# Two loads moved behind a DMA turning, the last remainder tile moved behind a visit's groups, and output banks dealt by element, in a fused attention and two-layer kernel on one Trainium2 core

## The chip, the cores and the metric

The kernel runs on one core of one Trainium2 chip. The metric is the device time of one execution in microseconds (us). The core has a matrix engine, TensorE (PE in the profile, its weight loads PEld), and three more that compute: VectorE (DVE), ScalarE (ACT) and GpSimd (POOL). SyncE (SP) only issues DMAs. POOL issues DMAs too. Each engine works through its own list of instructions in order and waits on semaphores for the others. PE writes its results to PSUM, which has eight banks; DVE and ACT read them there.

## The reference

The kernel computes an attention with normalised queries and keys and passes the result through two matrix products with a leaky ReLU between them.

```python
# batch 8, heads 12, sequence 448, head size 64; d_model 768, d_ff 2048
q_n = q / (np.linalg.norm(q, axis=-1, keepdims=True) + 1e-06)
k_n = k / (np.linalg.norm(k, axis=-1, keepdims=True) + 1e-06)
scores = np.matmul(q_n, k_n.transpose(0, 1, 3, 2)) / tau          # tau = 0.1
scores = scores - np.max(scores, axis=-1, keepdims=True)
attn = np.exp(scores)
attn = attn / (np.sum(attn, axis=-1, keepdims=True) + 1e-09)
attn_out = np.matmul(attn, v)
x = attn_out.transpose(0, 2, 1, 3).reshape(3584, 768)
h = x @ w_in                                                       # 768 x 2048
out = np.maximum(0.01 * h, h) @ w_out                              # 2048 x 768
```

## The kernel before

**Units of work.** The 12 heads of a batch entry are taken two at a time: a pair s, six to a batch entry, 48 in all. A pair's 448 positions are three full tiles of 128 and a remainder of 64. The remainders of two neighbouring pairs share one tile. Two pairs make an element j, three elements to a batch entry. The two matrix products go over chunks of tokens: two batch entries are 896 columns, cut into a chunk of 384 (three tiles of 128, the even chunks) and one of 512 (four tiles, the odd chunks). There are eight chunks.

**A pair's way.** `load_qk(s)` issues four DMAs from SyncE (two of 192 KB, two of 32 KB) into one of four buffers. `squares(s)` squares them on GpSimd, behind `hold`, a one-element copy that makes GpSimd wait until a given pair has been normalised. `sums(s)` reduces the squares on VectorE, `roots(s)` takes the root on ScalarE, `normalise(s)` multiplies on VectorE. `transposes(s)` turns the pair: by PE for s below 10, and from s = 10 on (`DMA_FROM`) with one transposing DMA from SyncE, L259, into one of five buffers `qkT`. `norm(s)` is roots, normalise and transposes, and then the loads of a later pair, the hold, and the squares of pair s + 2.

**A chunk's way.** `firsts(b)` multiplies chunk b by `w_in` (L388) and ScalarE applies the leaky ReLU (L395), giving `hT`. Then `visit(b)` multiplies `hT` by `w_out` (L460) in `two_groups`: two output groups at once, in the two row halves of the PE array, 2 x 16 steps `n` of one pair of matmuls, into the two banks of a bank pair; VectorE then copies both banks out (L470), and SyncE stores the tile when both of its halves are there. Between these steps `visit` places the score tiles of batch entry b + 1 (`key_tiles`, L284, each into a bank pair, exponential on ScalarE, L296): the schedules `three` and `four` say after which step of a group a tile comes. A remainder tile (`ki == 3`) is made of four matmuls in 64 x 64 parts of the array. Two of the three remainder tiles of a batch entry stand ahead of the groups, the last one right after the last full tile, inside the last `two_groups`. After the visit, `attend_batch(b + 1)` computes the attention: `attend_two` for two elements together (remainder parts first, L311, in 64 x 32 parts of the array; then totals and products, L324, 128 x 32), `attend` for the third. `reciprocals` (L343, L344) are on ScalarE, `scale` (L365) on VectorE; its output xT is what the next `firsts` multiplies.

**What sets the order.** The order is written out by hand (`manual_schedule`): every engine gets its instructions in the order of the calls. Semaphores are put in by the framework. SyncE's DMAs take eight completion counters in turn, so each DMA also waits until the one eight before it has landed. Banks are dealt by `banks`: of the pairs that are not kept, the one whose last deal or return is the oldest. In `two_groups` the pair is kept until its copies are issued.

In the visit of chunk 0, the attention's batch entry 1 is being prepared, and the pairs of batch entry 2 begin to be loaded: `norm(10)` comes at the end of `firsts(0)` and `norm(11)` after step 26 of the first `two_groups`.

Of the kernel before, what the change touches and what calls it, by code (L numbers as in the profile page):

```python
# [16 lines left out]
def kernel(  # L17
# [10 lines left out]
    nc = tc.nc  # L28
# [10 lines left out]
    NQ = NPAIR // 2  # L39
    KT = D_model // 128  # L40
    MT = D_ff // 128
    HALF = D_model // 2
# [33 lines left out]
    def banks(count, keep=None, which=None):  # L76
        lo, hi = (0, 8) if not deals["apart"] else (0, 4) if count == 2 else (4, 8)
        x = which if which is not None else min(
            (i for i in range(lo, hi, count) if not set(range(i, i + count)) & set(sum(kept.values(), []))),
            key=lambda i: max(age[i : i + count]),  # L80
        )
        deals["n"] += 1
        age[x : x + count] = [deals["n"]] * count
        if keep:
            kept[keep] = list(range(x, x + count))
        return ps[:, x] if count == 1 else ps[:, x : x + count]
# [31 lines left out]
    def main(x, b, h0, nh):  # L118
        return x[b, h0 : h0 + nh, 0:MAIN].rearrange("h (p t) d -> p h t d", t=3)
# [19 lines left out]
    def load_qk(s):  # L139
        if s >= NSLOT:  # L140
            return
        b, h0 = s // NPAIR, 2 * (s % NPAIR)
        both = ldp.tile([128, 2, 7, D], F32, name="qk")
        nc.sync.dma_start(out=both[:, :, 0:3], in_=main(q, b, h0, 2))
        nc.sync.dma_start(out=both[:, :, 4:7], in_=main(k, b, h0, 2))
        for i, x in enumerate((q, k)):
            nc.sync.dma_start(
                out=both[64 * i : 64 * i + 64, :, 3],
                in_=x[b, h0 : h0 + 2, MAIN:S].rearrange("h p d -> p h d"),
            )  # L150
        raw[s] = (both[:, :, 0:4], both[:, :, 4:7])
# [23 lines left out]
    def squares(s, engs=(gp, gp)):  # L175
        if s >= NSLOT:
            return
        tiles = []
        for x, eng, name in zip(raw[s], engs, ("sq0", "sq1")):
            sq = sqp.tile(list(x.shape), F32, name=name)  # L180
            if eng is nc.scalar:
                nc.scalar.activation(sq, x, func=AF.Square)
            else:
                eng.tensor_tensor(sq, x, x, op=ALU.mult)  # L184
            tiles.append(sq)
        sqs[s] = tiles
# [22 lines left out]
    def behind(eng, ins, why):  # L209

        tc.add_manual_dep(
            eng.nop().ins, ins.ins.name,
            mybir.DependencyInfo(mybir.DependencyClass.Sync, mybir.DependencyReason.DATA),
            reason=why,
        )
# [56 lines left out]
    def key_tiles(which):  # L272

        tiles = []
        for s, ki in which:
            sc = banks(2)
            tiles.append(sc)
            for i in range(2 if ki == 3 else 1):
                x = qkT[s - 1 + (i ^ s // 2 % NQ % 2)] if ki == 3 else qkT[s]
                for a in range(2):  # L280
                    rows = slice(64 * a, 64 * a + 64)
                    out = sc[64 * i : 64 * i + 64] if ki == 3 else sc
                    c0, c1 = (448, 512) if ki == 3 else (512 + 128 * ki, 640 + 128 * ki)
                    nc.tensor.matmul(  # L284
                        out=out[:, a, :S], lhsT=x[rows, c0:c1], rhs=x[rows, 0:S],
                        start=True, stop=True,
                    )
        for (s, ki), sc in zip(which, tiles):
            if ki == 3:
                pr[s // 2] = prp.tile([128, 2, S], BF16, name="pr")  # L290
                dst = pr[s // 2]
            else:
                if s not in pe:
                    pe[s] = pep.tile([128, 3, 2, S], BF16, name="pe")
                dst = pe[s][:, ki]
            nc.scalar.activation(out=dst, in_=sc[:, :, :S], func=AF.Exp, scale=inv_tau)  # L296
# [52 lines left out]
    def products(j, e, po=None, begun=False):  # L349
        b, jj = divmod(j, NQ)  # L350
        if po is None:
            po = banks(1, (j, e))
        pos[j, e] = po
        vm = vb[j].rearrange("p h t (d e) -> p h t e d", e=2)
        vr = vrb[b % 2].rearrange("p j g (d e) -> p j g e d", e=2)
        strip_products(
            j, po, lambda g, ki: vm[:, g, ki, e], None if begun else lambda g: vr[:, jj, g, e]
        )
# [15 lines left out]
    def chunk_cols(c):  # L374
        return (0, MAIN) if c % 2 == 0 else (MAIN, 512)
# [25 lines left out]
    osb = {}  # L401
# [41 lines left out]

    halves_done = {}

    def two_groups(c, two):

        po2 = banks(2, ("rows", c, two))  # L450
        last = {}
        for n in range(2):
            before, last = last, {}
            for m in range(MT):
                for h in range(2):
                    rows, i = slice(64 * h, 64 * h + 64), h ^ n
                    ts, half = two[i]
                    if n == 1 and m == 0:
                        behind(nc.tensor, before[i], "the other rows' products in this bank")
                    last[i] = nc.tensor.matmul(  # L460
                        out=po2[:, i, :HALF],
                        lhsT=hT[c][rows, m, ts * 128 : (ts + 1) * 128],
                        rhs=w_out_sb[rows, m, half * HALF : (half + 1) * HALF],
                        start=(n == 0 and m == 0), stop=(n == 1 and m == MT - 1),
                    )
                yield
        for i, (ts, half) in enumerate(two):
            if (c, ts) not in osb:
                osb[c, ts] = osp.tile([128, D_model], F32, name="osb")
            nc.vector.tensor_copy(  # L470
                out=osb[c, ts][:, half * HALF : (half + 1) * HALF], in_=po2[:, i, :HALF]
            )
            halves_done[c, ts] = halves_done.get((c, ts), 0) + 1
            if halves_done[c, ts] == 2:
                store(osb[c, ts], c, chunk_cols(c)[0] + ts * 128, 0, D_model)
        given_back(("rows", c, two))
# [38 lines left out]
    def hold(x):  # L515
        seen = smp.tile([128, 1], F32, name="seen")
        gp.tensor_copy(out=seen, in_=x)  # L517
# [154 lines left out]
    def attend_two(j):  # L672
        two = (j, j + 1)
        sm = banks(2)
        po = [banks(2) for _ in two]
        vr = vrb[j // NQ % 2].rearrange("p j g (d e) -> p j g e d", e=2)
        rem_products(two, [sm[:, i] for i in range(2)], lambda j, g, rows: ones[rows])
        for e in range(2):
            rem_products(
                two, [x[:, e] for x in po], lambda j, g, rows, e=e: vr[rows, j % NQ, g, e]  # L680
            )
        for i, j in enumerate(two):
            totals(j, sm[:, i])
        for j, x in zip(two, po):
            for e in range(2):
                products(j, e, x[:, e], True)
            for e in range(2):
                scale(j, e)

# [11 lines left out]
    def norm(s, transposed=True):  # L701
        if s >= NSLOT:
            return
        roots(s)
        normalise(s)
        if transposed:
            transposes(s)
        if 9 <= s < 12:
            load_qk(s + 2)
        elif s not in (7, 8):  # L710
            load_qk(s + 4)
        hold(qn[s][:, 6, 0, 0:1])
        squares(s + 2)

    def firsts(b, begun, between):
# [9 lines left out]
    def visit(b, order, norms, between):  # L725


        s0 = (b + 1) * NPAIR
        tiles = [(s0 + p, ki) for p in range(NPAIR) for ki in range(3)]
        key_tiles([(s0 + 1, 3), (s0 + 3, 3)])  # L730
        for i, two in enumerate(order):
            after = between[i == len(order) - 1]
            for n, _ in enumerate(two_groups(b, two), 1):
                for _ in range(after.get(n, 0)):
                    key_tiles([tiles.pop(0)])
                if not tiles and s0 + 5 not in ended:
                    ended.add(s0 + 5)
                    key_tiles([(s0 + 5, 3)])
                for fn in norms.get((i, n), ()):
                    fn()  # L740
        assert not tiles

    ended = set()
    three = ({5: 1, 11: 1, 16: 2, 21: 1, 27: 1}, {3: 1, 7: 1, 11: 1, 16: 2, 20: 1})
    four = ({5: 1, 11: 1, 16: 2, 24: 1}, {6: 1, 16: 2})

# [17 lines left out]
    for b in range(B):  # L764
# [6 lines left out]
        order = [((ts, 0), (ts, 1)) for ts in range(tokens)]  # L771
        if b == 0:
            order = [((0, 0), (1, 0)), ((2, 0), (0, 1)), ((1, 1), (2, 1))]
# [12 lines left out]
        s = ready  # L786
# [57 lines left out]
```

## Time and profile before

| what | value |
| --- | --- |
| median of 3 runs | 411.54 us (411.3 to 411.54) |
| the profiled execution | 411.49 us, of it 409.7 us from first to last instruction |
| PE busy | 400.1 us, 98% of the span |
| ACT, DVE, POOL busy | 259.0, 193.4 and 140.7 us |
| L388, products with w_in | 148.1 us in 768 matmuls |
| L460, products with w_out in `two_groups` | 143.3 us in 1536 matmuls of half the rows |
| L284, scores | 54.8 us in 384 matmuls |
| L470, copies of `two_groups` on VectorE | 48, 552 ns each |
| DMA turnings, L259 | 38, median 3.0 us from issue to landing |

A busy time of PE is not PE at its peak: records of matmuls overlap, and matmuls in different parts of the array run together. The columns of the order of time, shown below, are: start in us from the span's start, duration, engine, line, operation, what it writes and reads, sizes, how many; in brackets how long the engine was idle before it, and what ended that.

### The profile page before, as it was taken

How to read it: one execution, taken by the hardware profiler on the slowest of the kernel's cores; microseconds unless marked ns; L12 is line 12 of the kernel's file. 1: busy time of each engine (PE TensorE's matmuls, PEld its weight loads, DVE VectorE, ACT ScalarE, POOL GpSimd, SP SyncE). 2: the span in 40 equal slices, each digit the busy share in tenths (PEclk: the TensorE clock that was granted, in tenths of full speed). 3: DMA queues.
4: the chain of work that ended last, by engine and by line, in shares of the span. 5: the costliest groups of instructions: out<-in, count | busy, mean ns of one | idle time of the engine just before them, and what ended most of it. 6: DMA issues, size and time to landing. Idle time of an engine off the chain costs nothing.

```text
span 409.7 us, 10108 instructions
## 1 busy us (share of the span) xinstructions
PE 400.1 (98%) x4096; PEld 213.8 (52%) x4096; DVE 193.4 (47%) x412; ACT 259.0 (63%) x448; POOL 140.7 (34%) x216
## 2 busy tenths in 40 slices
PE   7899998999999999999999999999999999999996
PEld 3335655544555655544555555544555555554564
DVE  5987850762644734365453625257261645130021
ACT  4996597546865579745875569745775559844300
POOL 4995461282323423254140624055231530000000
PEclk9999999999999999999999999999999999999999
DMA  7999999596495839277485868587385833210023
GB/s 170 263 214 217 221 178 205 169 179 160 109 202 94 152 77 195 84 114 156 107 186 122 120 139 141 132 113 136 92 194 126 119 82 63 62 41 2 0 77 78
DMA packets 104175, 54.21 MB, mean 132 GB/s; under 512 B 70016, under 2 KB 99072, under 8 KB 104128
## 3 DMA queue, kind: packets, MB, share of 16 engines
q1 hardware_dynamic: 78064, 41.04, 44.1%
q0 software_dynamic: 25216, 12.00, 22.8%
q8 instruction: 32, 0.52, 0.6%
q10 hardware_dynamic: 848, 0.52, 0.4%
q14 instruction: 15, 0.12, 0.1%
HBM read 45.61 MB, written 11.01 MB: 138 GB/s over the span
## 4 chain that ended last, share of the span: by engine, by line
PE 82%; DMA 11%; POOL 3%; DVE 1%; issue 1%; ACT 0%; POOLq 0%
PE ps L388 32%; PE ps L460 28%; PE ps L324 10%; DMA w_out_sb<-in_moe_w_out_dram 7%; PE ps L284 6%; PE ps L425 5%; DMA raw<-in_k_dram 2%; DMA qkT<-qn 2%; POOL sq L184 2%; PE ps L311 1%; DVE qn L227 1%; POOL w_out_sb L113 1%; DVE r L223 0%; POOL seen L517 0%; POOL w_in_sb L106 0%
## 5 line engine op out<-in xcount | busy, mean ns | idle before, releaser
L388 PE MATMUL ps<-xT,w_in_sb 128*128 128x384 bf16 (+1 forms) x768 | 148.1, 353 | 0.0
L460 PE MATMUL ps<-w_out_sb,hT 64*128 64x384 bf16 x1536 | 143.3, 323 | 0.3 <-DMA w_out_sb<-in_moe_w_out_dram 0.3
L296 ACT ACTIVATE pe<-ps 128x896 bf16<-128x896 f32 x144 | 123.3, 919 | 21.7 <-PE ps L284 20.0
L388 PEld LDWEIGHTS <-w_in_sb 128*128 128x128 bf16 x768 | 74.1, 98 | 71.8 <-issue 4.0
L395 ACT ACTIVATE hT<-ps 128x384 bf16<-128x384 f32 (+1 forms) x128 | 67.3, 543 | 69.6 <-PE ps L388 69.2
L460 PEld LDWEIGHTS <-hT 64*128 64x128 bf16 x1536 | 74.7, 94 | 54.8 <-issue 4.0
L184 POOL TENSOR_TENSOR sq<-qk 128x512 f32<-128x512 f32 x84 | 77.1, 939 | 18.0 <-DMA qk<-in_k_dram 17.0
L470 DVE COPY osb<-ps 128x384 f32<-128x384 f32 x48 | 24.5, 552 | 78.4 <-PE ps L460 45.2
L284 PE MATMUL ps<-qkT 64*128 64x448 bf16 (+1 forms) x384 | 54.8, 354 | 3.2 <-DMA qkT<-qn 1.6
L195 DVE TENSOR_REDUCE ss<-sq 128x6 f32<-128x384 f32 (+1 forms) x95 | 54.5, 610 | 3.0 <-POOL sq L184 2.9
L517 POOL CAST seen<-qn 128x1 f32<-128x1 bf16 x48 | 9.0, 188 | 130.0 <-DVE qn L227 125.3
L227 DVE TENSOR_TENSOR qn<-qk,r 128x512 bf16<-128x512 f32 x84 | 50.5, 642 | 2.0 <-DVE r L223 0.6
L222 DVE TENSOR_SCALAR ss<-ss 128x14 f32<-128x14 f32 x46 | 10.5, 227 | 66.9 <-ACT ss L203 66.8
L365 DVE TENSOR_TENSOR xT<-ps,rb 128x448 bf16<-128x448 f32 x48 | 27.7, 619 | 20.5 <-ACT rb L344 20.3
L162 POOL DMA_DIRECT2D v_b<-in_v_dram x24 | 18.7, 784 | 54.2 <-PE ps L324 54.2
L324 PE MATMUL ps<-pe,v_b 128*32 128x448 bf16 x576 | 32.0, 353 | 0.0
L284 PEld LDWEIGHTS <-qkT 64*128 64x128 bf16 (+1 forms) x384 | 17.0, 96 | 22.8 <-issue 8.8
L343 ACT ACTIVATE rb<-ps 128x448 f32<-128x448 f32 x24 | 12.9, 537 | 22.2 <-PE ps L324 21.2
L431 DVE COPY osb<-ps 128x384 f32<-128x384 f32 (+1 forms) x9 | 4.6, 512 | 36.6 <-issue 22.6
L296 ACT ACTIVATE pr<-ps 128x896 bf16<-128x896 f32 x24 | 21.3, 922 | 0.2 <-PE ps L284 0.2
L324 PEld LDWEIGHTS <-v_b 128*32 128x32 bf16 x576 | 15.2, 97 | 11.8 <-issue 0.6
L425 PE MATMUL ps<-w_out_sb,hT 128*128 128x384 bf16 (+1 forms) x144 | 21.0, 308 | 0.0
(51 smaller groups left out, 196.2 us busy)
## 6 DMA issues: line engine op xcount, KB each, us to landing
qk<-in_q_dram SPq DMA_DIRECT2D x42, 192.0 KB, 3.4
qk<-in_k_dram SPq DMA_DIRECT2D x42, 192.0 KB, 3.4
out_dram<-osb SPq DMA_DIRECT2D x30, 192.0 KB, 3.0
v_b<-in_v_dram POOLq DMA_DIRECT2D x24, 192.0 KB, 4.9
out_dram<-osb SPq DMA_DIRECT2D x12, 384.0 KB, 2.7
w_in_sb<-in_moe_w_in_dram POOLq DMA_DIRECT2D x4, 768.0 KB, 11.8
w_out_sb<-in_moe_w_out_dram POOLq DMA_DIRECT2D x2, 768.0 KB, 21.8
w_out_sb<-in_moe_w_out_dram POOLq DMA_DIRECT2D x4, 384.0 KB, 25.2
```

Source lines behind the costliest of these rows:

```text
L184: eng.tensor_tensor(sq, x, x, op=ALU.mult)
L195: nc.vector.tensor_reduce(o.rearrange("p (h t) -> p h t", h=2), sqs[s][i], axis=AX.X, op=ALU.add)
L227: scalings[s] = nc.vector.tensor_tensor(qn[s][:, lo:hi], x.rearrange("p h t d -> p t h d"), r[:, r0 : r0 + 2 * nt].rearrange("p (h t) -> p ...
L284: nc.tensor.matmul(out=out[:, a, :S], lhsT=x[rows, c0:c1], rhs=x[rows, 0:S], start=True, stop=True,)
L296: nc.scalar.activation(out=dst, in_=sc[:, :, :S], func=AF.Exp, scale=inv_tau)
L324: nc.tensor.matmul(out=x[32 * g : 32 * g + 32, :S], lhsT=weights(g, ki) if ki < 3 else rem(g), rhs=pe[s][:, ki, a, :] if ki < 3 else pr[j] ...
L365: nc.vector.tensor_tensor(xT[m][:, 2 * jj + e, half * S : (half + 1) * S], pos.pop((j, e))[:, :S], rbs[j], op=ALU.mult,)
L388: nc.tensor.matmul(out=pm[:, :n], lhsT=w_in_sb[:, kt, m * 128 : (m + 1) * 128], rhs=xT[c // 2][:, kt, c0 : c0 + n], start=(kt == 0), stop= ...
L395: nc.scalar.activation(out=hT[c][:, m, :n], in_=pms.pop((c, m))[:, :n], func=AF.Prelu, alpha=0.01)
L425: nc.tensor.matmul(out=po2[:, :n], lhsT=hT[c][:, m, ts * 128 : (ts + 1) * 128], rhs=w_out_sb[:, m, lo : lo + n], start=(m == 0), stop=(m = ...
L460: last[i] = nc.tensor.matmul(out=po2[:, i, :HALF], lhsT=hT[c][rows, m, ts * 128 : (ts + 1) * 128], rhs=w_out_sb[rows, m, half * HALF : (ha ...
L470: nc.vector.tensor_copy(out=osb[c, ts][:, half * HALF : (half + 1) * HALF], in_=po2[:, i, :HALF])
```

## The change

**Loads.** `norm(10)` ends after the turning of pair 10: its loads of pair 12, its hold and its squares of pair 12 are left out there. `norm(11)` then loads pairs 12 and 13 one after the other, behind the turning of pair 11, and squares pair 12 ahead of pair 13. One hold is left out for good.

**Remainder tile.** The last remainder tile of a visit, which stood inside the last `two_groups`, comes behind all groups of the visit, after the last copies have been issued and the bank pair is back in the deal. It holds for the seven visits.

**Copies.** In the last `two_groups` of a visit, the first of the two copies is made by ScalarE and the second by VectorE; before, VectorE made both.

**Banks in `attend_two`.** Of the two bank pairs for products, one held both halves e of the first element and the other those of the second. Now one holds half e = 0 of both elements and the other half e = 1 of both.

```diff
-    def two_groups(c, two):
+    def two_groups(c, two, last):
...
-            nc.vector.tensor_copy(
-                out=osb[c, ts][:, half * HALF : (half + 1) * HALF], in_=po2[:, i, :HALF]
-            )
+            copy = nc.scalar.copy if last and i == 0 else nc.vector.tensor_copy
+            copy(out=osb[c, ts][:, half * HALF : (half + 1) * HALF], in_=po2[:, i, :HALF])
...
-        po = [banks(2) for _ in two]
+        po = [banks(2) for e in range(2)]
...
             rem_products(
-                two, [x[:, e] for x in po], lambda j, g, rows, e=e: vr[rows, j % NQ, g, e]
+                two, [po[e][:, i] for i in range(2)], lambda j, g, rows, e=e: vr[rows, j % NQ, g, e]
             )
...
-        for j, x in zip(two, po):
+        for i, j in enumerate(two):
             for e in range(2):
-                products(j, e, x[:, e], True)
+                products(j, e, po[e][:, i], True)
...
-        if 9 <= s < 12:
-            load_qk(s + 2)
+        if s == 10:
+            return
+        if s == 11:
+            load_qk(12)
+            load_qk(13)
         elif s not in (7, 8):
-            load_qk(s + 4)
+            load_qk(s + (2 if s == 9 else 4))
         hold(qn[s][:, 6, 0, 0:1])
+        if s == 11:
+            squares(12)
         squares(s + 2)
...
-            for n, _ in enumerate(two_groups(b, two), 1):
+            for n, _ in enumerate(two_groups(b, two, i == len(order) - 1), 1):
                 for _ in range(after.get(n, 0)):
                     key_tiles([tiles.pop(0)])
-                if not tiles and s0 + 5 not in ended:
-                    ended.add(s0 + 5)
-                    key_tiles([(s0 + 5, 3)])
                 for fn in norms.get((i, n), ()):
                     fn()
         assert not tiles
+        key_tiles([(s0 + 5, 3)])
```

More of the change, by code (lines that the diff above doesn't have):

```diff
@@ L444 @@
     halves_done = {}
-    def two_groups(c, two):
+    def two_groups(c, two, last):
         po2 = banks(2, ("rows", c, two))
-        last = {}
+        done = {}
         for n in range(2):
-            before, last = last, {}
+            before, done = done, {}
             for m in range(MT):
@@ L459, in two_groups @@
                         behind(nc.tensor, before[i], "the other rows' products in this bank")
-                    last[i] = nc.tensor.matmul(
+                    done[i] = nc.tensor.matmul(
                         out=po2[:, i, :HALF],
@@ L741, in visit @@
         assert not tiles
-    ended = set()
+        key_tiles([(s0 + 5, 3)])
     three = ({5: 1, 11: 1, 16: 2, 21: 1, 27: 1}, {3: 1, 7: 1, 11: 1, 16: 2, 20: 1})
```

## The prediction, made before the changed kernel was run

> **What bounds the kernel now.** I read the page's first two parts, then the waits, then the order of time around the one long wait, then the order of time at the end of an ordinary visit. By the page, TensorE (PE) works 400.1 of 409.7 us at the full granted clock; the other engines are far from full, and DMA is full only in the first 70 us.
>
> ```profile
> span 409.7 us, 10108 instructions
> PE 400.1 (98%) x4096; PEld 213.8 (52%) x4096; DVE 193.4 (47%) x412; ACT 259.0 (63%) x448; POOL 140.7 (34%) x216
> PE   7899998999999999999999999999999999999996
> PEclk9999999999999999999999999999999999999999
> DMA  7999999596495839277485868587385833210023
> ```
>
> So only what leaves PE idle can be won. Of the waits that end a PE idle time, the longest is a single one, for a DMA turning (the transpose of L259):
>
> ```profile
> PE ps L284 <- DMA qkT<-qn: 1.6, 1, 1.6
> PE ps L508 <- DVE warm L491: 1.5, 1, 1.5
> ```
>
> The second is the start-up, which the change leaves alone. The first stands in the visit of chunk 0. I call pair s's four loads "loads s" and its turning "turning s" (s counts from 0: the 12th pair is s = 11). SPq is SyncE's queue:
>
> ```profile
> 53.19 1.35 SPq L259 DMA_TRANSPOSE qkT<-qn  x1
> 54.65 0.51 SPq L144 DMA_DIRECT2D qk<-in_q_dram  x1
> ...
> 56.49 0.70 SPq L147 DMA_DIRECT2D qk<-in_k_dram  x1
> ...
> 59.57 2.64 SPq L259 DMA_TRANSPOSE qkT<-qn  x1
> ...
> 66.31 1.82 POOL L184 TENSOR_TENSOR sq<-qk 128x512 f32<-128x512 f32 x2 [6.35 <-DMA qk<-in_k_dram]
> 66.89 1.11 PE L460 MATMUL ps<-w_out_sb,hT 64*128 64x384 bf16 x10
> 69.62 0.55 PE L284 MATMUL ps<-qkT 64*128 64x448 bf16 x4 [1.61 <-DMA qkT<-qn]
> 71.68 1.82 POOL L184 TENSOR_TENSOR sq<-qk 128x512 f32<-128x512 f32 x2 [3.43 <-DMA qk<-in_k_dram]
> ```
>
> Turning 10 goes out at 53.19, loads 12 behind it, turning 11 at 59.57. By the tile's view both turnings land 9.9 to 10.0 us after their issue: 63.1 and 69.6. The squares of s = 12 start at 66.31, when loads 12 have landed. PE needs turning 11 when its last pair ends: the record of a matmul is about 0.16 us longer than the pace at which the next one follows, so PE could have gone on at 68.00 - 0.16 = 67.85 and loses 69.62 - 67.85 = 1.77 us.
>
> The end of an ordinary visit (chunk 1):
>
> ```profile
> 122.41 0.85 PE L284 MATMUL ps<-qkT 64*128 64x448 bf16 x8
> 122.88 0.11 PEld L284 LDWEIGHTS <-qkT 64*64 64x64 bf16 x4 [0.37 <-issue]
> 123.20 2.77 PE L460 MATMUL ps<-w_out_sb,hT 64*128 64x384 bf16 x32
> 125.91 0.38 PE L311 MATMUL ps<-pr,ones 64*32 64x448 bf16 x8
> 126.07 1.02 DVE L470 COPY osb<-ps 128x384 f32<-128x384 f32 x2 [5.22 <-ACT pr L296]
> 126.11 0.56 PE L311 MATMUL ps<-pr,v_rem 64*32 64x448 bf16 x16
> 126.60 1.32 PE L324 MATMUL ps<-pe,ones 128*32 128x448 bf16 x24
> ```
>
> Tiles that lie beside each other in the array run together as a set. A set of 448 columns takes 0.19 us (an L284 pair at 120.60, L460 at 120.79, both in 64*128), a pair of 384 columns 0.163. What is more than that is lost where the array's tile shape changes: two L284 pairs (0.38) begin at 122.41, the remainder tile (64*64) at 122.88: 0.09 lost. From there to L460 it is 0.32, 0.13 lost. Sixteen L460 pairs take 2.60 and end at 125.80, L311 begins at 125.91: 0.10 lost.
>
> **The change part by part.**
>
> *Loads behind the turning.* In the built program SyncE's order is turning 10, turning 11, loads 12, loads 13, the first store. Turning 11 still waits for its normalised rows (SyncE's wait ended at 59.5 on DVE), so it goes out at 59.57. What changes is what lies ahead of it in the queue: turning 10 (landed 63.1) in place of loads 12 (landed 66.2). It landed 69.6 - 66.2 = 3.4 us after the work ahead; behind turning 10 that gives 63.1 + 3.4 = 66.5, which is 1.35 us before PE wants it. Bounds: 3.0 us after issue (the page's median of 38 turnings), and 9.9 us, turning 10's own time, though loads 11, ahead of it, had landed by 53.2. I take 66.5, whose row is the same turning in the same traffic: the wait goes, -1.77 us. [...]
>
> What moves: four DMAs of loads 12 (2.5 us of issue) and four of loads 13, from 54.65 and 62.31 to 62.3 and 64.8 or so, and the first store (65.93) behind them, to about 67.3 or when loads 12 have landed, whose completion counter it reuses. The output tile that this store empties is wanted again at 107.5. Loads 12 then land where they stood behind turning 10 before, 3.1 us after the turning: 69.6, loads 13 at 71.5 as now, since the queue holds the same work. POOL loses one 0.26 us cast (the hold of s = 10) and squares s = 12 at 69.7 to 71.5. VectorE sums them after its last copy, at about 71.9 in the new time (74.5 now), and its next work, the first scaling (76.06 now, about 74.2 then), waits for ScalarE anyway. So loads 12 may land at 71.7 with no effect, and PE is reached 1.5 us beyond that (the four scalings end at 78.35, L388 starts at 79.85). If this cover went, each us would cost one. The remainder rows of v, third of four transfers, landed at 70.5; attention will want them at 73.56 - 1.77 - 0.12 = 71.7: cover 1.2 us, same price.
>
> *Remainder tile behind the groups*, seven visits. Three changes of shape (0.09 + 0.13 + 0.10 = 0.32) become two: into 64*64 (0.09 to 0.10) and from 64*64 to 64*32, which this trace does not have. Its nearest rows are the changes beside it, 0.09 to 0.13; zero is the lower end. I take 0.10: 0.20 in all, -0.12 a visit, -0.84 us. [...] ScalarE's exponential of this tile moves behind the groups too (0.92 us); it is wanted by the totals of the third element, some 4.6 us later, and the logarithm of the first totals comes 2.1 us after the last pair has begun, when that exponential has ended (0.37 + 0.49 + 0.93 = 1.8). Cover 0.3 us; beyond it ScalarE would delay the scalings, which have 1.5 us of their own.
>
> *Banks dealt by element, one copy on ScalarE.* The oldest banks now go to the remainder tile, so the third set of L311 (element half e = 1) falls on the banks that the last group has just filled: a new wait of PE, for a copy on ScalarE and one on VectorE. Count from the start of the last L460 pair, 125.65: PE comes to that set after 0.163 + 0.10 (into 64*64) + 0.19 + 0.10 (into 64*32) + 0.20 + 0.19 = 0.94. VectorE's copy starts at 126.07 (0.42) and takes 0.55 (552 ns is the mean of L470); PE follows DVE after 0.06 (a DVE copy ended 24.88, PE started 24.94): 1.03. ScalarE's copy is not in the trace; the nearest row, L395 of the same 128x384, has 490 ns, and ScalarE starts 0.05 after PE's record ends (0.32): 0.37 + 0.49 + 0.05 = 0.91. ScalarE is free then (its last exponential before ends 0.9 us or more earlier, once the remainder's is gone). So PE waits 0.09; bounds 0 (if the changes of shape are 0.13) and 0.15 (if ScalarE's copy is like L554's 585 ns). I take 0.08, +0.56 us in seven visits. Queued behind it on PE is all of the attention.
>
> Scaling order and xT are the same; VectorE saves a copy a visit where it is idle (5.2 us before it), which is worth nothing.
>
> **Sum.** The profiled execution took 411.49 us, 0.05 below the median of 411.54. 411.49 - 1.77 - 0.84 + 0.56 = 409.44 us. A difference of under 0.2% (0.82 us) is about what can't be told from none.
>
> **Rivals.**
> (a) The turning stays late. Turning 10 took 9.9 us with no load ahead; if POOL's loads of v set the pace of turning 11 as well, it lands at 69.4, PE still loses about 1.6, and 411.49 - 0.15 - 0.28 = 411.1 is left, no change. Against it: POOL's big weight loads, beside which turning 10 ran, end at 60.6. 15%.
> (b) The seven bank waits cost more than the seven changes of shape save, by up to 0.15 - 0.09 = 0.06 each: +0.4, and with the turning's gain 410.1. 8%.
> (c) Slower: the two copies read two banks of one pair and exclude each other. Then the second ends 0.49 after VectorE's, PE waits 0.57 a visit, and 411.49 - 1.77 + 7 x (0.57 - 0.12) = 412.9. It is slower than before by more than can be missed from a wait of 0.12 + 2.6/7 = 0.49 on. Against it: VectorE's two copies take 1.02 at 59.43 with ScalarE's exponentials beside them, and 1.02 at 126.07 alone. 7%, with the late loads of s = 12 in it.
> That the change does not do what it says is excluded by the built order of the instructions.
>
> **How the numbers follow.** The forecast has 70%: 409.4, by itself 408.6 (unseen change of shape free, no bank wait) to 410.0. With (a) and (b) the range goes to 411.2 and leaves out (c), a part of (a), and a little below: 408.5 to 411.2. Faster by over 0.2%: the forecast, (b) and part of (a), 0.77; within 0.2%: most of (a), 0.15; slower: (c) and the unforeseen, 0.08.
>
> **What would show it.** The wait of PE for qkT gone or under 0.3 us, and the last pairs of chunk 0's visit 1.8 us earlier; squares of s = 12 at about 69.7. At each visit's end: no 0.3 us step inside the L460 run, L311 starting 0.29 us after the remainder tile, and a PE wait for a copy of L471 near 0.1 us. Wrong if turning 11 lands after 67.9, if the wait for L471 is 0.3 or more, or if a wait for loads 12 or the remainder rows of v appears near 72 us.

## The result, and the profile after

The changed kernel took 409.44 us (median of 6 runs, 408.97 to 409.81), the kernel before 411.56 beside it (6 runs, 411.3 to 413.47). The ratio is 0.9938, its 95% interval 0.9918 to 0.9957. The forecast was 409.4 us, counted from 411.49 for the profiled execution of before; that of after took 408.97, its span 407.2.

First, from the page of the changed kernel: span, busy times, the 40 slices of PE, of its clock and of DMA (each digit is the share of one slice, in tenths), and the chain of work that ended last.

```profile
span 407.2 us, 10112 instructions
PE 399.3 (98%) x4096; PEld 216.3 (53%) x4096; DVE 189.8 (47%) x405; ACT 262.6 (64%) x455; POOL 140.7 (35%) x215
PE   7899999999999999999999999999999999999996
PEclk9999999999999999999999999999999999999999
DMA  7999999694595659378385848486476833210033
PE 93%; DMA 3%; DVE 1%; POOL 1%; SPq 1%; issue 0%
```

PE is still the bound. The dip of its seventh slice (8 before) is gone. Next PE's longest waits (us in total, how many, the longest):

```profile
PE ps L507 <- DVE warm L490: 1.5, 1, 1.5
PE ps L241 <- DVE qn L227: 0.9, 2, 0.7
PE ps L284 <- ACT pe L296: 0.9, 3, 0.5
PE ps L284 <- DVE qkT L265: 0.6, 2, 0.3
```

The wait for `qkT` (1.6 before) is not among them, and a second one is missing too, which the prediction did not show. It was for the last part of `w_out` and ended at 60.68 us, some 8 us ahead of the turning's wait. In the list of waits and in the order of time of before:

```profile
PE ps L460 <- DMA w_out_sb<-in_moe_w_out_dram: 0.3, 1, 0.3
...
60.68 0.81 PE L460 MATMUL ps<-w_out_sb,hT 64*128 64x384 bf16 x7 [0.29 <-DMA w_out_sb<-in_moe_w_out_dram]
```

All the waits of PE that are left in the list of after stand before 52 us.

The order of time of after, around the turning:

```profile
59.82 1.73 SPq L259 DMA_TRANSPOSE qkT<-qn  x1
61.65 0.53 SPq L144 DMA_DIRECT2D qk<-in_q_dram  x1
...
66.74 1.10 PE L460 MATMUL ps<-w_out_sb,hT 64*128 64x384 bf16 x10
67.51 0.60 SPq L147 DMA_DIRECT2D qk<-in_k_dram  x1
67.55 0.66 PE L284 MATMUL ps<-qkT 64*128 64x448 bf16 x4
68.21 4.17 SPq L440 DMA_DIRECT2D out_dram<-osb  x3
69.53 1.82 POOL L184 TENSOR_TENSOR sq<-qk 128x512 f32<-128x512 f32 x2 [9.46 <-DMA qk<-in_k_dram]
72.08 1.82 POOL L184 TENSOR_TENSOR sq<-qk 128x512 f32<-128x512 f32 x2 [0.73 <-DMA qk<-in_k_dram]
```

Five L460 pairs of 0.163 us from 66.74 end at 67.55, and there L284 begins: nothing is lost. But turning 11 landed only at 67.49 (7.7 us after its issue, by the tile's view), 0.06 us ahead of PE. The squares of s = 12 start at 69.53 (forecast about 69.7), the first store goes out at 68.21 (the first of loads 12, eight of SyncE's DMAs ahead of it, had landed at 68.13), and no wait of PE for either follows.

The order of time of after at the end of an ordinary visit (chunk 1 again):

```profile
120.67 2.76 PE L460 MATMUL ps<-w_out_sb,hT 64*128 64x384 bf16 x32
123.36 0.38 PE L284 MATMUL ps<-qkT 64*64 64x448 bf16 x4
123.50 0.48 ACT L471 COPY osb<-ps 128x384 f32<-128x384 f32 x1 [1.09 <-PE ps L460]
123.52 0.56 DVE L471 COPY osb<-ps 128x384 f32<-128x384 f32 x1 [4.79 <-issue]
123.68 0.38 PE L311 MATMUL ps<-pr,ones 64*32 64x448 bf16 x8
123.88 0.64 PE L311 MATMUL ps<-pr,v_rem 64*32 64x448 bf16 x16
124.44 1.32 PE L324 MATMUL ps<-pe,ones 128*32 128x448 bf16 x24
```

The sixteen L460 pairs now follow the full tile without a step. The change into the remainder tile costs 123.36 - 120.67 - 2.60 (the sixteen pairs) = 0.09 us, that from 64*64 to 64*32, which before did not have, 123.68 - 123.36 - 0.19 = 0.13. The two copies start 0.02 us apart on two engines. From the v_rem products to L324 it is 0.56 us, 0.49 before (126.11 to 126.60): 0.07 us of waiting for a bank. It is too short and too well covered by overlapping records to appear in the list of waits.

Where the 2.48 us of span went in this pair of profiles, read at the first instruction of each line in each visit, after less before:

| stage | us |
| --- | --- |
| up to the first L460 of visit 0 | +0.31 |
| visit 0: the turning's wait | -1.77 |
| visit 0: the wait for w_out | -0.45 |
| visit 0: the rest (changes of shape, no bank wait) | -0.21 |
| six more visits, changes of shape (0.10 to 0.16 each) | -0.79 |
| six more visits, bank wait (0.07 to 0.08 each) | +0.45 |
| the end | -0.02 |

A wait is given "by pace": the time between two starts on PE less the pace of what ran between. That is about 0.16 us more than the idle time that the list of waits shows, since a matmul's record (L460: 323 ns, the mean) outlasts its pace (163 ns).

### The profile page after: what moved, and what is told of

Same layout as the page of the kernel before. It is cut to its first block, busy times and chain, and to the rows that moved or that the text cites. A ratio compares the mean times of both kernels' runs of the same rounds, so it can differ in the third digit from the quotient of the medians.

```text
span 407.2 us, 10112 instructions
## 1 busy us (share of the span) xinstructions
PE 399.3 (98%) x4096; PEld 216.3 (53%) x4096; DVE 189.8 (47%) x405; ACT 262.6 (64%) x455; POOL 140.7 (35%) x215
## 4 chain that ended last, share of the span: by engine, by line
PE 93%; DMA 3%; DVE 1%; POOL 1%; SPq 1%; issue 0%
PE ps L388 36%; PE ps L460 31%; PE ps L324 11%; PE ps L284 8%; PE ps L425 5%; DMA raw<-in_k_dram 2%; PE ps L311 1%; DMA raw<-in_q_dram 1%; DMA qk<-in_q_dram 1%; DVE qn L227 1%; PE ps L241 1%; POOL sq L184 1%; DVE ss L195 0%; SPq L129 0%; SPq L134 0%
## 5 line engine op out<-in xcount | busy, mean ns | idle before, releaser
L460 PE MATMUL ps<-w_out_sb,hT 64*128 64x384 bf16 x1536 | 143.2, 323 | 0.0
L395 ACT ACTIVATE hT<-ps 128x384 bf16<-128x384 f32 (+1 forms) x128 | 67.4, 543 | 70.1 <-PE ps L388 69.7
L460 PEld LDWEIGHTS <-hT 64*128 64x128 bf16 x1536 | 76.4, 94 | 52.9 <-issue 2.7
L284 PE MATMUL ps<-qkT 64*128 64x448 bf16 (+1 forms) x384 | 55.1, 354 | 1.6 <-ACT pe L296 0.9
L471 DVE COPY osb<-ps 128x384 f32<-128x384 f32 x41 | 21.3, 553 | 72.9 <-PE ps L460 42.4
L222 DVE TENSOR_SCALAR ss<-ss 128x14 f32<-128x14 f32 x46 | 9.9, 214 | 67.9 <-ACT ss L203 67.8
L324 PE MATMUL ps<-pe,v_b 128*32 128x448 bf16 x576 | 32.0, 353 | 0.0
L284 PEld LDWEIGHTS <-qkT 64*128 64x128 bf16 (+1 forms) x384 | 17.0, 96 | 20.5 <-issue 8.5
L324 PEld LDWEIGHTS <-v_b 128*32 128x32 bf16 x576 | 15.1, 97 | 11.9 <-issue 0.6
```

The source lines that it names most:

```text
L284: nc.tensor.matmul(out=out[:, a, :S], lhsT=x[rows, c0:c1], rhs=x[rows, 0:S], start=True, stop=True,)
L324: nc.tensor.matmul(out=x[32 * g : 32 * g + 32, :S], lhsT=weights(g, ki) if ki < 3 else rem(g), rhs=pe[s][:, ki, a, :] if ki < 3 else pr[j] ...
L395: nc.scalar.activation(out=hT[c][:, m, :n], in_=pms.pop((c, m))[:, :n], func=AF.Prelu, alpha=0.01)
L460: done[i] = nc.tensor.matmul(out=po2[:, i, :HALF], lhsT=hT[c][rows, m, ts * 128 : (ts + 1) * 128], rhs=w_out_sb[rows, m, half * HALF : (ha ...
L471: copy(out=osb[c, ts][:, half * HALF : (half + 1) * HALF], in_=po2[:, i, :HALF])
```

## The experiments

Medians stand beside those of the kernel before, run on the same chip at the same time.

**The changed kernel again.** No edit.

> The changed kernel once more, for the spread. In its first profile turning 11 landed at 67.49 us and PE wanted it at 67.55, so the cover was 0.06 us. If that is so in general, PE's wait for qkT comes and goes by some tenths of a us between executions, and the times spread over about 409.0 to 409.8 us as before. If the landing is repeatable to 0.1 us, the profile shows the same and the spread has another cause.

409.72 us (409.0 to 410.45, 7 runs) beside 411.48 (30 runs): ratio 0.9952, its 95% interval 0.9934 to 0.997. Its profiled execution took 410.45, 1.48 more than the first. Two of PE's waits in it:

```profile
PE ps L241 <- DVE qn L227: 1.3, 3, 0.8
...
PE ps L460 <- DMA w_out_sb<-in_moe_w_out_dram: 0.7, 1, 0.7
```

The start was 0.56 us later than in the first profile of after (0.87 later than before's), and the last part of `w_out` landed at 61.92 in place of 60.46, which cost 0.87 us by pace. Turning 11 went out at 60.39 and landed at 68.81, later than the 67.9 that I had named as the limit; but PE, late itself, came to it at 68.99. The two waits stand 8 us apart in one visit: what PE loses at the first it does not lose at the second.

**The loads alone.** The kernel before, with this edit only:

```diff
-        if 9 <= s < 12:
-            load_qk(s + 2)
+        if s == 10:
+            return
+        if s == 11:
+            load_qk(12)
+            load_qk(13)
         elif s not in (7, 8):
-            load_qk(s + 4)
+            load_qk(s + (2 if s == 9 else 4))
         hold(qn[s][:, 6, 0, 0:1])
+        if s == 11:
+            squares(12)
```

> Only the loads moved behind turning 11; tile, copies and banks as before. My theory: the 1.77 us wait for turning 11 goes and nothing else moves: 411.56 - 1.8 = 409.8 us, turning 11 at about 67.5, and the changes of shape at the visits' ends stay at 0.34 us each. Rival, that most of the gain comes from the tile and the banks: 411 us.

410.04 us (409.22 to 412.01, 12 runs) beside 411.48: 0.997, interval 0.9956 to 0.9984, that is -1.44 by medians. The profiled execution was the slowest of the twelve; PE's list of waits in it begins:

```profile
PE ps L460 <- DMA w_out_sb<-in_moe_w_out_dram: 2.1, 1, 2.1
PE ps L508 <- DVE warm L491: 1.5, 1, 1.5
```

`w_out` landed at 62.98 there and PE lost 2.24 us by pace. Turning 11 landed at 68.64 and PE, not there before 70.05, did not wait. From the end of visit 0 to the end of the kernel this execution stands 0.56 us behind the first profile of before at every stage: the loads edit touches nothing outside visit 0. It had started visit 0 as late, by 0.56; inside the visit what it won at the turning (1.77) it lost at `w_out` (2.24 in place of 0.45). So the gain of the edit is the turning's wait, as far as PE would have been there to wait.

**Tile, copy and banks alone.** The changed kernel with the loads put back as they were:

```diff
-        if s == 10:
-            return
-        if s == 11:
-            load_qk(12)
-            load_qk(13)
+        if 9 <= s < 12:
+            load_qk(s + 2)
         elif s not in (7, 8):
-            load_qk(s + (2 if s == 9 else 4))
+            load_qk(s + 4)
         hold(qn[s][:, 6, 0, 0:1])
-        if s == 11:
-            squares(12)
```

> Only the remainder tile, the copy on ScalarE and the banks; loads as before. My theory: turning 11 lands at 69.6 and PE waits about 1.8 us as before; each visit's end gains 0.12 by one change of shape less and loses about 0.07 by the bank wait, so 411.56 - 0.4 = 411.1 us. Rival, that the visits carry the gain: under 410.3 us.

410.81 us (409.84 to 412.84, 12 runs) beside 411.48: 0.9986, interval 0.9971 to 1.0, -0.67 by medians. The interval reaches 1.0, so the times alone do not show this gain; in the profile the six later visits gave -0.35 us, as in the whole change. Two of PE's waits show how visit 0 shares a delay between them:

```profile
PE ps L460 <- DMA w_out_sb<-in_moe_w_out_dram: 0.8, 1, 0.8
...
PE ps L284 <- DMA qkT<-qn: 0.4, 1, 0.4
```

By pace 0.94 and 0.53, where the first profile of before had 0.45 and 1.77. The parts add up within what the sets differ by: -1.44 and -0.67 make -2.11, the whole gave -2.12, -1.76 and, further down, -1.84.

**A load of v behind the squares.** To take POOL's last load of `v` out of turning 11's way I moved it behind `norm(11)`:

```diff
-            13: [lambda: load_v(5), lambda: load_v_rem(1)],
+            13: [lambda: load_v_rem(1)],
...
-        norms = {(0, 16): [lambda: sums(11)], (0, 26): [lambda: norm(11)]}
+        norms = {(0, 16): [lambda: sums(11)], (0, 26): [lambda: norm(11), lambda: load_v(5)]}
```

> The changed kernel with the load of v's element 5 (192 KB from POOL) issued behind the 11th index pair's normalising (about 60 us in place of 56.6), and the remainder rows of v ahead of it. If POOL's loads share the DMA engines with turning 11, the turning lands 0.5 to 1 us earlier (66.5 to 67.0), PE never waits for it, and the median falls to about 409.0 us when the edge is what spreads the changed kernel's times, or stays at 409.4 when not. If POOL's loads do not matter to it, the landing stays at 67.5.

413.06 us (410.79 to 416.6, 12 runs) beside 411.48: 1.0041, interval 1.0017 to 1.0066, slower. Turning 11 did land earlier, 6.2 us after its issue, at 66.17. But on POOL the load of `v` now stood behind the squares of s = 12 and 13, which waited for their own loads: it went out only at 72.67, and attention came to it too early. The order of time:

```profile
76.23 0.36 PE L324 MATMUL ps<-pr,ones_rem 128*32 128x448 bf16 x4
78.50 0.75 PE L324 MATMUL ps<-pe,v_b 128*32 128x448 bf16 x12 [1.91 <-DMA v_b<-in_v_dram]
```

The run answers the question on the landing and, for its time, only shows what such a place in the queue costs.

**Banks as before.** The changed kernel with the two bank pairs dealt by element of the batch, as they were:

```diff
-        po = [banks(2) for e in range(2)]
+        po = [banks(2) for _ in two]
...
-                two, [po[e][:, i] for i in range(2)], lambda j, g, rows, e=e: vr[rows, j % NQ, g, e]
+                two, [po[i][:, e] for i in range(2)], lambda j, g, rows, e=e: vr[rows, j % NQ, g, e]
...
-                products(j, e, po[e][:, i], True)
+                products(j, e, po[i][:, e], True)
```

> The changed kernel with the banks of the two-element attention dealt by element j as before, tile and copies as changed. The second set of L311 (half 0) then already falls on the bank that ScalarE's copy empties, 0.19 us earlier than with the new deal. My theory: PE comes there 0.75 us after the last pair's start and the copy is done at 0.91, so PE waits about 0.17 a visit in place of 0.07: +0.6 us, 410.0 us. Rival, that the deal does not matter: 409.4 us.

410.14 us (409.68 to 410.81, 5 runs) beside 411.58 (9 runs): 0.9966, interval 0.9952 to 0.9979. The order of time at chunk 1's end:

```profile
125.18 0.72 PE L311 MATMUL ps<-pr,v_rem 64*32 64x448 bf16 x16
125.83 1.32 PE L324 MATMUL ps<-pe,ones 128*32 128x448 bf16 x24
```

0.65 us in place of 0.56: the bank wait is 0.16 where the new deal has 0.07. The same comes out in all six later visits, which together give +0.17 where the whole change has -0.34. So without the deal by element the moved tile would have cost more than it saves there.

**Both copies on VectorE.** The changed kernel with

```diff
-            copy = nc.scalar.copy if last and i == 0 else nc.vector.tensor_copy
+            copy = nc.vector.tensor_copy
```

> The changed kernel with both last copies on VectorE. The second copy ends at 0.42 + 0.48 + 0.55 = 1.45 us after the last pair's start, PE follows at 1.51 and wants the bank at 0.94: a wait of 0.57 in place of 0.07 in each of seven visits, +3.4 us: 412.8 us, slower than before. Rival, that this wait is hidden by something: 409.4 us.

413.2 us (412.89 to 413.44, 4 runs) beside 411.58: 1.004, interval 1.0027 to 1.0054. The order of time at chunk 1's end:

```profile
124.60 1.02 DVE L471 COPY osb<-ps 128x384 f32<-128x384 f32 x2 [4.80 <-issue]
124.75 0.38 PE L311 MATMUL ps<-pr,ones 64*32 64x448 bf16 x8
124.95 1.11 PE L311 MATMUL ps<-pr,v_rem 64*32 64x448 bf16 x16
125.99 1.32 PE L324 MATMUL ps<-pe,ones 128*32 128x448 bf16 x24
```

1.04 us from the v_rem products to L324, so 0.55 of waiting (0.57 expected), in each of seven visits. This is the price that my slower rival (c) had named for two copies that exclude each other. Paid seven times it is large enough to make the whole change a loss; the changed kernel does not pay it, since its two copies run side by side.

**A part of loads 12 left ahead.** The first 192 KB of loads 12 issued ahead of turning 11, the rest behind:

```diff
...
+            load_qk(12, first_only=True)
             return
         if s == 11:
             load_qk(12)
```

> The changed kernel with the first 192 KB of the 13th pair's 448 KB left ahead of turning 11, the rest behind. If what stands ahead in SyncE's queue sets the landing, turning 11 lands part of the way back from 67.5 to 69.6, by 192/448 at about 68.4, and PE waits about 0.9 us; time about 410.3 us. If it is not the queue, it lands at 67.5 and the time is 409.4 us.

410.44 us, one run, beside 411.58. Turning 11 landed 9.3 us after its issue, at 68.99, and PE waited for it. From PE's waits (the added lines move L284 to L290):

```profile
PE ps L290 <- DMA qkT<-qn: 1.0, 1, 1.0
```

By pace 1.12 us (0.9 expected). With nothing of loads 12 ahead, turning 11 took 7.6 to 8.5 us from issue to landing in the other kernels with POOL's loads in place, with all four of them ahead 9.3 to 10.0. By this one run, then, one load of 192 KB ahead costs some 0.8 to 1.7 us: what is ahead in its own queue does hold a turning back.

**No loads of v.** The loads of `v` for the second batch entry left out (the first one's tiles are used again):

```diff
+        if NQ <= j < 2 * NQ:
+            vb[j] = vb[j - NQ]
+            return
...
-        if b >= B:
+        if b >= B or b == 1:
```

> The changed kernel without the loads of v for the second batch entry (three of 192 KB and four of the remainder rows); the attention of that entry reads the first entry's v in their place. If turning 11 only follows what is ahead of it in its own queue, it lands 3.4 us after turning 10, at about 66.5. If POOL's loads set its pace, as turning 10's 9.9 us suggest, it lands at 64.5 us or earlier. The time stays near 409.4 us in both cases, since PE does not wait for it.

409.33 us, one run. The tile's view of its two turnings (added lines make L259 L262), the answers of two stretches one behind the other, turning 10 first; the last three numbers are the least, the median and the greatest time to landing:

```profile
L262 SPq DMA_TRANSPOSE qkT<-qn x1: 1358/1358/1358, 53.5 to 53.5; - x1
DMA to landing us min/median/max: 7.8/7.8/7.8
...
L262 SPq DMA_TRANSPOSE qkT<-qn x1: 2367/2367/2367, 59.9 to 59.9; - x1
DMA to landing us min/median/max: 3.6/3.6/3.6
```

In the changed kernel's first profile these are 9.7 and 7.7 us. Turning 11 landed at 63.44, 4 us earlier, with the same work ahead of it in its queue; 1.8 of the 4 us turning 10 had already gained. So POOL's loads, not only what is ahead, set when it lands: rival (a) had its reason right. It had its result wrong, since in the first profile even 7.7 us was enough.

Where turning 11 loses this time shows in the changed kernel's first profile. SyncE's queue moved turning 10's last packet at 62.44 us and the next one, turning 11's first, at 64.52. In between only POOL's queue (q0) moved anything. The view of DMA from 62.5 to 64.5 us:

```profile
DMA packets 1025, 0.38 MB, mean 189 GB/s; under 512 B 1025, under 2 KB 1025, under 8 KB 1025
q0 software_dynamic: 1025, 0.38, 160.6%
```

In the nine profiles with nothing of loads 12 ahead and POOL's loads in place, two of them with one load of `v` elsewhere, this stretch lasts 1.3 to 2.6 us. Without the loads of `v` it is not there, and turning 11 landed 2.1 us behind turning 10 in place of 4.3.

**Two ways on.** With `w_out` as what is left to wait for, I let one group of chunk 0 multiply its last quarter after the other group's work, so that the last part of `w_out` is wanted later:

```diff
+        passes = [(0, range(MT)), (1, range(MT))]
+        if c == 0 and two == ((2, 0), (0, 1)):
+            passes = [(0, range(12)), (1, range(MT)), (0, range(12, MT))]
...
```

> The changed kernel; in the second group of chunk 0's visit the last quarter of w_out's rows (m = 12 to 15) is multiplied at the end of the group in place of the middle of it, in both passes, so PE wants the last load of w_out about 1.95 us (12 pairs) later, at the price of one more hand-over between the row halves. In seven profiles so far that load landed between 60.5 and 63.0 us and PE waited for it 0 to 2.2 us. My theory now, that this wait is what spreads the times: it goes, turning 11 is wanted earlier and PE may wait some tenths for it; 409.0 us, and a narrower spread. Rival, that the wait only moves to turning 11: 409.5 us.

409.26 us (409.03 to 409.79, 6 runs) beside 411.4 (10 runs): 0.9949, interval 0.9937 to 0.9962. `w_out` landed at 61.87 and PE did not wait for it; in the old order it would have come to it after two pairs more, at 59.85 + 2 x 0.163 = 60.18, and lost some 1.7 us. The median stayed above the 409.0 expected. This order has two changes between the row halves of the array, and they cost 0.23 us each, where the one that they replace stands behind two score tiles and cost nothing (61.02 + 2 x 0.19 = 61.40 in the first profile of after).

In a second kernel I also put the last load of `v` on POOL right behind the hold of the 12th pair, ahead of the squares, where it does not wait for them:

```diff
         if s == 11:
+            load_v(5)
             squares(12)
...
-            13: [lambda: load_v(5), lambda: load_v_rem(1)],
+            13: [lambda: load_v_rem(1)],
```

> As the run before, and the load of v's element 5 behind the 12th pair's hold, ahead of its squares on POOL, so that turning 11 shares the DMA engines with less: it landed at 66.2 us with that load away, 67.5 with it. Element 5 should land by 71 us and is wanted at about 76. Both waits of chunk 0's visit gone: 408.8 us. Rival, that element 5 comes too late as in the run with it behind the squares: over 410 us.

409.13 us (409.01 to 410.21, 6 runs; 408.8 expected): 0.995, interval 0.9937 to 0.9963. Turning 11 landed at 67.55 as without this edit, where 66.2 was expected. Beside both ran the changed kernel once more:

> The changed kernel beside the two, for the comparison on one chip: 409.4 to 409.7 us; the start and the landing of the last load of w_out differ from those of the first profile by some tenths, the ends of the visits do not.

409.56 us (409.07 to 410.23, 6 runs): 0.9954, interval 0.9942 to 0.9965. In its profile PE lost 0.41 us by pace for `w_out`, and 0.24 us for turning 11, which landed at 68.79: the cover of 0.06 us can fail. The two kernels' medians are 0.30 and 0.43 us lower, but all three intervals overlap, and 0.1% is less than can be told here. They beat the kernel before; that they beat the changed one is not shown.

**The kernel before, profiled again.**

> The kernel before, one more profile. If the wait for w_out varies in it as in the others, the wait for turning 11 is the smaller the longer that one is, since the turning does not start later: their sum stays near 2.2 us or rises, and the moved loads are worth less than 1.77 us where w_out comes late.

412.61 us, one run. PE lost nothing for `w_out`, which landed at 59.85, and 2.08 us by pace for the turning, landed at 69.09. That is the other end of the exchange between the two waits. Their sum is 2.08 here and 2.22 in the first profile of before; that it stays there, as expected, does not hold in general, since tile, copy and banks alone had 0.94 + 0.53 = 1.47. But PE's clock also fell to 0.50 after that wait, which is told under the surprises.

## Why the prediction was right, and where it was not

**The total.** 409.4 forecast; 409.44, 409.72 and 409.56 measured in three sets. The gain was forecast as 2.05 us and came as 2.12, 1.76 and 1.84 by medians. In the pair of profiles compared above the turning's part came in its full size, and the span fell by 2.48: two terms that I did not have, the wait for `w_out` (-0.45) and the start (+0.31), stand in it too. That the medians lie within 0.3 us of the forecast is in part luck, since what the turning's wait is worth in an execution hangs on the wait for `w_out`, which the sum left out.

**The turning's wait, -1.77.** Gone, as forecast, and put back in part by one load ahead of it (1.12 us). The step that failed is the landing time, "66.5, which is 1.35 us before PE wants it". It was 67.49 in the first profile, 68.81 and 68.79 in the two others of the same kernel, both later than the 67.9 that I had named as a sign of being wrong. I took the delay behind the work ahead in its queue (3.4 us) from before, where that work was loads 12, and laid it behind turning 10. Measured behind turning 10 it was 4.3, 5.8 and 5.8 us. The runs show why: ahead of the turning's first packet, SyncE's queue stood still for 2.1 to 2.6 us in these three profiles while POOL's moved its loads. What is ahead in the queue counts as well (0.8 to 1.7 us for 192 KB, one run), but that the change had taken away.

POOL's loads take time from the turnings: with the loads of `v` away, turning 10 took 7.8 us instead of 9.7 and turning 11 took 3.6 instead of 7.7. How they do it is not the same in every stretch. From 62.5 to 64.5 us in the first profile of before, SyncE's queue, with loads 12 in it, moved 418 packets beside 393 of POOL's. In these same two microseconds of after, with a turning next in it, it moved none beside 1025; and in before, from 53.3 to 57 us, with turning 10 next in it, none beside 1008. Why a turning had no packet at all there stays open.

My sum was saved by the size of the cover, of which 0.06 us was left in the first profile; in the third PE lost 0.24 us.

Loads 12 came when forecast, but by two errors that cancel: they landed at 69.37 (69.6 forecast), 1.9 us behind a late turning and not 3.1 behind an early one.

**What was left out.** The wait for the last part of `w_out`, 8 us ahead of the turning's wait. Its landing moved between 59.85 and 62.98 us over these executions, and it cost 0 to 2.24 us by pace, 0.45 in the profile that I read. Together with the start (0.26 us earlier to 0.93 later than in that profile) it makes the executions of one kernel differ by over 1 us (408.97, 410.45 and 410.23 in the three profiles of the changed kernel). It also sets the worth of the loads edit: where PE is late from it, the turning's wait is shorter. Alone the edit gave -1.44 by medians and not -1.77. What moves the landing of `w_out` is not settled.

**The changes of shape, -0.84.** -0.79 in six visits and up to -0.21 in visit 0. The unseen change from 64*64 to 64*32 costs 0.13 us; I had taken 0.10 from its neighbours. None of the changes priced in these profiles was free (0.09 to 0.13 us each), so the lower end of zero for the unseen one was out. With zero there the seven visits would have saved 7 x (0.32 - 0.10) = 1.54 us and the lower end of the forecast would have been 411.49 - 1.77 - 1.54 = 408.2; the 408.6 in the prediction does not follow from its two conditions.

**The bank wait, +0.56.** 0.45: 0.07 to 0.08 in six visits where I had 0.08, none in visit 0 of the first profile, where VectorE's copy began 0.06 us after the remainder tile (0.16 in chunk 1's visit). That is not so in every execution: in the third profile visit 0 had 0.09. The terms behind it held: ScalarE's copy 478 ns (490 taken), VectorE's 557 (0.55). Its upper bound, 0.15 with a ScalarE copy of 585 ns, was wrong by my own count: that copy would be done at 0.37 + 0.585 + 0.05 = 1.0, and VectorE's at 1.03 would still end the wait. Without the deal by element the wait is 0.16.

**The rivals.** (a), the late turning, had the mechanism but not the time: 7.7 to 8.4 us in place of 9.9. (b) did not come: the bank wait stayed under what the changes of shape save. (c) did not come; with both copies on VectorE its price was 0.55 us a visit, 0.57 forecast. Loads 12 and 13 and the store behind the turning cost nothing, as forecast: PE's list has no wait for them, and the first scaling after visit 0 came at 73.94 (about 74.2 forecast).

## What to carry to other kernels

Work out a moved transfer's landing from all the loads that run beside it, other queues' too (turning 11 took 7.7 us with POOL's loads of `v` beside it, 3.6 without), and look at the cover that is left, not only at the wait that goes: here 1.8 us were won, in one profile, with 0.06 us to spare. Waits that lie near each other on the bounding engine can share one delay (0.45 and 1.77 us, 0.94 and 0.53, 0 and 2.08 in the three profiles with the loads where they were), so take each from several executions before pricing the removal of one. When work is moved to a place where banks have just been filled, the order in which the banks are dealt and the engines that empty them are part of the same change: either of them put back turned the six later visits from a gain into a loss.

## What was not expected of the hardware

After the wait for the turning in the kernel before, profiled again (2.08 us by pace, 1.92 idle), PE ran at half its clock (0.50 granted). The windows' columns are the stretch and its length, busy times of PE, PEld, DVE, ACT and POOL with their counts, PE's granted clock, DMA share, GB/s:

```profile
68.00:70.00 2.00, 0.86 (x10) 0.50 (x12) 0.00 (x0) 0.46 (x1) 0.00 (x0) 1.00 1.36 255
70.00:72.00 2.00, 2.00 (x20) 0.79 (x16) 0.00 (x0) 2.00 (x4) 0.83 (x1) 0.66 0.59 215
72.00:74.00 2.00, 2.00 (x16) 0.95 (x14) 0.00 (x0) 0.89 (x2) 0.99 (x2) 0.50 0.00 0
74.00:76.00 2.00, 2.00 (x52) 0.82 (x50) 1.30 (x3) 0.00 (x0) 0.00 (x0) 0.99 0.00 0
```

By these shares the clock was halved for (0.34 x 2 + 0.50 x 2 + 0.01 x 2) / 0.5 = 3.4 us. From the wait's end to the first L311, PE took 74.51 - 69.14 = 5.37 us, against 73.36 - 69.62 = 3.74 in the first profile: a wait of 2.08 us cost 1.63 more. It does not always follow: 2.08 us of idle time for `w_out`, in the profile of the loads alone, left the clock at 1.00, and so did the 1.61 us in the first profile of before.

What sets these cases apart may be where the gap falls. In the trace's record of the clock it was halved from 70.62 to 74.04 us, for 3.41 us, and the full stretches of the 13 other profiles last 399.36, 402.77 or 406.19 us, which differ by 3.41 us too: in these 14 records the clock changed only at whole steps of 3.41 us. Counted in them, the gap that cost the clock lay whole in one step. Of the 2.08 us at most 1.64 lay in one step, of the 1.91 us with the late load of `v` 1.57, of the 1.61 us 1.48, and these left the clock full. No one amount sorts all the cases: at the kernel's end 1.98 us of idle time in one step left the clock full in the run with the banks as before, and 2.06 us did not in the one with the late load of `v`. So that the share of a step decides is my guess, and is not shown.

The executions of the kernel with the late load of `v`, which idled 1.91 us in its profile, are the ones with most of it: 7 of 12 had a mean clock of 0.991 to 0.996, and the longest of them took 416.6 us. None of the 19 executions of the changed kernel was below 0.998. Whether removing such waits is worth more than their length was not measured by itself.
